# Attention and a two-layer MLP on one core: the sign of float64 weights through a Prelu, and two head pairs moved from TensorE

## The chip, the core and the metric

The kernel runs on one core of a Trainium2 chip. A core has TensorE (matrix products), VectorE, ScalarE and GpSimd (elementwise work and reductions), SyncE (it issues transfers) and 16 DMA engines. The time is device microseconds for one execution, as the median of several runs.

## What is computed

Attention with a causal mask over 4 batches, 12 heads, 448 tokens and 64 features per head, and then a two-layer MLP over the 1792 tokens. The weights `w_in` and `w_out` arrive as float64, because a float32 array was multiplied by a float64 scalar; q, k and v are float32.

```python
scores = scale * np.matmul(q, k.transpose(0, 1, 3, 2))
scores = np.where(np.triu(ones, k=1), -1e9, scores)
attn = np.exp(scores - np.max(scores, axis=-1, keepdims=True))
attn = attn / (np.sum(attn, axis=-1, keepdims=True) + 1e-09)
x = np.matmul(attn, v)                    # then (1792, 768)
h = x @ w_in                              # (1792, 2048)
out = np.maximum(0.01 * h, h) @ w_out     # (1792, 768)
```

## The kernel before

**Attention** goes by pairs of heads, 24 of them, numbered u = 0 to 23, six to a batch. For a pair, `features` brings k and q with features on partitions into a tile kq. Pairs below `TURNED` load whole rows, TensorE transposes them (line 402) and ScalarE copies the result out of PSUM (line 405). Later pairs load 32-column runs, four loads per tensor, and VectorE transposes blocks (line 394). `scores` multiplies on TensorE (lines 433 and 447, the second adds the mask). `softmax` takes the largest score of each query, which lies along partitions: ScalarE copies chunk 0 into M (line 468), VectorE takes maxima with the other three chunks (line 474, told by its helper as 251), GpSimd reduces over partitions into MR (line 476), VectorE subtracts (line 482), ScalarE takes Exp (line 489). `products` multiplies by v (line 500) and ScalarE copies the result to xu (line 506).

`finish(u)`, for every odd u, handles pairs u-1 and u. It sums the exponentials: below `ADDS` on TensorE against ones (line 520), from `ADDS` on by three adds per pair on VectorE (line 529) and a reduction per head on GpSimd (line 535). The sums go through small transfers on ScalarE's queue: to sc, to the reciprocal on VectorE (lines 546 and 547), to DRAM (scr), and back as broadcasts to rb. VectorE divides, rb = xu * rb (line 561), ScalarE takes the high part of the result (line 562) and VectorE the low part (line 563). Both parts of a batch's six pairs form the tile xt.

**Layer 1** takes three products per block, high x high, low x high, high x low, 18 per output block f and 288 per batch (line 585). ScalarE applies the leaky maximum with Prelu (line 591), and SyncE stores to DRAM as gd. **Layer 2** (line 772) reads gd back, 1176 products of 384 columns, with combined weights W and combined activations r (`combine`, lines 635 to 638).

**Weights.** `unpack` turns a float64, read as two 32-bit words, into a float32. ScalarE scales the high word, read as a float32, by 2^-112, which moves its exponent to where a shift by three bits keeps it. VectorE takes the sign from the high word (line 333), joins the top three bits of the low word to it (line 335), and shifts the scaled value left by three and joins that (line 337). It is called 16 times for `w_in`, beside attention, and 16 times for `w_out`, behind it. Each call covers 768 results per partition. A w_in value is then split into a high part wh (ScalarE, line 353) and a low part wl (VectorE, line 356).

**The order.** `Plan.emit` sets the order of all engines. It is a list scheduler with written-out durations that gives each operation a priority: the pair's number plus a number of its kind from the table `LATER`, and for the weights a line `PIECE`. Layer 1 has lower priority and fills TensorE between attention's operations; where nothing is ready TensorE gets small products on zeros (`warm`, line 321). Each engine then runs its own list strictly in order.

Of the kernel before, what the change touches and what calls it, by code (L numbers as in the profile page):

```python
# [8 lines left out]
F32 = mybir.dt.float32  # L9
# [8 lines left out]


LATER = {  # L20
    "add": 30.41, "load": 20.48, "v": 44.64, "transpose": 285.25, "features": 38.43, "scores": 30.1,
    "chunk 0": 20.56, "max": -46.8, "all max": -64.55, "subtract": 56.57, "exp": -39.38, "products": 1.84,
    "take products": 35.34, "sum all": 56.98, "sums": 1.62, "take sums": -46.21, "spread": 73.7, "invert": 43.51,
    "store": -0.31, "broadcast": 43.97, "divide": 93.42, "x hi": 58.73, "x lo": -27.08,
}

EARLY = 8

TURNED = 12

PORT = (0.78, 2.05)

PIECE = (168.2, -16.48)


SAME = -29.41


class Plan:
# [123 lines left out]
def attention_moe_kernel(  # L163
# [15 lines left out]
    nc = tc.nc  # L179
# [67 lines left out]
    def copy(out_, in_, n, r=(), w=(), prio=0.0, **kw):  # L247
        return act(n + 55, lambda: nc.scalar.activation(out=out_(), in_=in_(), func=kw.pop("func", ACTF.Copy), **kw), r, w, prio)
# [75 lines left out]
    def unpack(out_, in_, words, sign, val, R, G, V, prio, first, base, after=()):  # L324

        word = lambda j: words().bitcast(I32).rearrange("p (n t) -> p n t", t=2)[..., j]
        g = lambda: sign().bitcast(I32)
        v = lambda: val().bitcast(I32)  # L330
        dma(950, out_, in_, (base,), (R,), first, after=after)
        copy(val, lambda: word(1).bitcast(F32), DM, (R, base), (V,), prio, scale=2.0 ** -112)
        dve(DM, lambda: nc.vector.tensor_scalar(out=g(), in0=word(1), scalar1=-0x80000000, scalar2=None, op0=ALU.bitwise_and),
            (R, base), (G,), prio, 0.5, port=-1)
        dve(DM, lambda: nc.vector.scalar_tensor_tensor(
            out=g(), in0=word(0), scalar=29, in1=g(), op0=ALU.logical_shift_right, op1=ALU.bitwise_or), (R, base), (G,), prio, chain=0.03, port=-1)
        return dve(DM, lambda: nc.vector.scalar_tensor_tensor(
            out=v(), in0=v(), scalar=3, in1=g(), op0=ALU.logical_shift_left, op1=ALU.bitwise_or), (G, base), (V,), prio, chain=0.03, port=-1)

# [69 lines left out]

    order = sorted(segs)  # L410
    NTB, NM = 3, 2
    ADDS = 11
    MERGE = [lambda u: u >= 0, lambda u: u >= 99, lambda u: u >= 99]
    for tag, n, width_ in (("M", NM, S), ("MR", 1, S), ("t", NTB, 1024)):
        for i in range(n):
# [440 lines left out]
```

## Time and profile before

| | |
|---|---|
| median of 3 runs | 593.76 us (592.93 to 595.21) |
| the profiled execution | 595.98 us, of which 594.2 us are its span |
| mean granted TensorE clock | 0.996 |
| attention's last product ends | about 271.6 us into the span |
| layer 1's last product ends | about 385 us |

Layer 1's first products stand at 67.7 us, so from there to 271.6 us attention and layer 1 share TensorE. A row of a timeline gives the start, the duration of the merged instructions, the engine, the line and, in brackets, how long the engine had been idle and what released it. A row of a group gives busy time in total and the mean of one instruction.

### The profile page before, as it was taken

How to read it: one execution, taken by the hardware profiler on the slowest of the kernel's cores; microseconds unless marked ns; L12 is line 12 of the kernel's file. 1: busy time of each engine (PE TensorE's matmuls, PEld its weight loads, DVE VectorE, ACT ScalarE, POOL GpSimd, SP SyncE). 2: the span in 40 equal slices, each digit the busy share in tenths (PEclk: the TensorE clock that was granted, in tenths of full speed). 3: DMA queues.
4: the chain of work that ended last, by engine and by line, in shares of the span. 5: the costliest groups of instructions: out<-in, count | busy, mean ns of one | idle time of the engine just before them, and what ended most of it. 6: DMA issues, size and time to landing. Idle time of an engine off the chain costs nothing.

```text
span 594.2 us, 10308 instructions
## 1 busy us (share of the span) xinstructions
PE 578.8 (97%) x3747; PEld 508.5 (86%) x3747; DVE 462.7 (78%) x929; ACT 276.7 (47%) x447; POOL 162.2 (27%) x82
## 2 busy tenths in 40 slices
PE   8989899999999999999999999999999999999997
PEld 7655667878777787788999999989999999999997
DVE  4899889999999887784167899999767666666664
ACT  3778566555543543434233546654423242424331
POOL 1544234353669887897000000000000000000000
PEclk9999899999999999999999999999999999999999
DMA  8976876688556664312388766105533333232201
GB/s 168 239 182 124 175 160 189 212 190 245 141 112 125 151 131 97 94 49 94 109 312 295 258 221 201 63 17 147 154 98 99 97 99 105 90 119 77 88 14 40
DMA packets 153486, 82.90 MB, mean 140 GB/s; under 512 B 95580, under 2 KB 151388, under 8 KB 153436
## 3 DMA queue, kind: packets, MB, share of 16 engines
q1 hardware_dynamic: 146304, 76.57, 46.6%
q10 hardware_dynamic: 7132, 5.68, 3.7%
q8 instruction: 29, 0.48, 0.3%
q14 instruction: 21, 0.17, 0.1%
HBM read 61.87 MB, written 20.27 MB: 138 GB/s over the span
## 4 chain that ended last, share of the span: by engine, by line
PE 69%; DVE 15%; issue 4%; ACT 3%; DMA 3%; POOL 3%; ACTq 1%; SPq 1%; DVEq 0%; POOLq 0%
PE h L772 32%; PE h L585 27%; PE big L500 4%; PE S L433 4%; DVE M L251 3%; DVE t L482 3%; POOL MR L476 2%; DVE W L638 2%; DVE v L635 2%; DVE t L251 2%; DMA qraw<-in_q_dram 1%; DMA rb<-scr 1%; ACTq L245 1%; SPq L245 1%; DVE r L638 1%
## 5 line engine op out<-in xcount | busy, mean ns | idle before, releaser
L585 PE MATMUL h<-xt,wh 128*128 128x448 f32 x768 | 221.9, 370 | 0.5 <-DVE xt L251 0.5
L772 PE MATMUL h<-W,r 128*128 128x384 f32 x882 | 164.1, 334 | 0.1
L772 PEld LDWEIGHTS h<-W,r 128*128 128x128 f32 x882 | 153.8, 188 | 0.6 <-DVE r L638 0.4
L585 PEld LDWEIGHTS h<-xt,wh 128*128 128x128 f32 x768 | 142.5, 189 | 13.0 <-DVE xt L251 0.8
L585 PE MATMUL h<-xt,wl 128*128 128x448 f32 x384 | 140.5, 366 | 0.0
L476 POOL PARTITION_ALL_REDUCE MR<-M x48 | 80.0, 1714 | 98.7 <-DVE M L251 75.2
L535 POOL PARTITION_ALL_REDUCE t<-t x28 | 81.7, 2964 | 18.3 <-DVE t L251 14.4
L585 PEld LDWEIGHTS h<-xt,wl 128*128 128x128 f32 x384 | 72.3, 188 | 5.8
L637 ACT ACTIVATE r<-v 128x512 fp32r<-128x512 f32 x70 | 41.9, 598 | 74.3 <-DVE v L635 74.1
L482 DVE TENSOR_TENSOR t<-S,MR 128x64 f32<-128x64 f32 x192 | 67.6, 410 | 2.2 <-POOL MR L476 2.2
L638 DVE TENSOR_TENSOR r<-v,r 128x512 fp32r<-128x512 f32 x70 | 47.2, 690 | 27.4 <-ACT r L637 25.7
L489 ACT ACTIVATE t<-t 128x1024 f32<-128x1024 f32 x48 | 50.6, 1056 | 33.3 <-DVE t L482 31.5
L251 DVE TENSOR_TENSOR M<-S,M 128x320 f32<-128x320 f32 x144 | 49.0, 354 | 20.2 <-ACT M L468 10.5
L772 PE MATMUL h<-xw,r 128*128 128x384 f32 x294 | 62.5, 335 | 0.6 <-DVE r L638 0.3
L591 ACT ACTIVATE h<-h 128x448 f32<-128x448 f32 x64 | 34.3, 538 | 55.0 <-PE h L585 33.7
L433 PE MATMUL S<-kq 64*128 64x192 f32 (+3 forms) x384 | 53.1, 404 | 4.3 <-DVE t L482 4.1
L772 PEld LDWEIGHTS h<-xw,r 128*128 128x128 f32 x294 | 51.9, 188 | 1.5 <-DVE r L638 1.0
L433 PEld LDWEIGHTS S<-kq 64*128 64x128 f32 x384 | 32.9, 186 | 23.0 <-issue 11.9
L500 PE MATMUL big<-t,v 128*64 128x192 f32 (+3 forms) x384 | 47.8, 386 | 0.8 <-ACT kq L405 0.8
L635 DVE TENSOR_TENSOR v<-A 128x512 f32<-128x512 f32 x71 | 47.7, 689 | 0.0
L500 PEld LDWEIGHTS big<-t,v 128*64 128x64 f32 x384 | 26.3, 136 | 22.0 <-issue 11.7
L637 ACT ACTIVATE r<-A 128x512 fp32r<-128x512 f32 x28 | 17.7, 632 | 30.3 <-PE h L772 30.3
(87 smaller groups left out, 520.0 us busy)
## 6 DMA issues: line engine op xcount, KB each, us to landing
gd<-h SPq DMA_DIRECT2D x64, 224.0 KB
A<-gd SPq DMA_DIRECT2D x28, 512.0 KB
stage<-in_moe_w_in_dram SPq DMA_DIRECT2D x16, 768.0 KB
A<-in_moe_w_out_dram SPq DMA_DIRECT2D x16, 768.0 KB
rb<-scr ACTq DMA_DIRECT2D x48, 112.0 KB
v<-in_v_dram SPq DMA_DIRECT2D x48, 96.0 KB
kraw<-in_k_dram SPq DMA_DIRECT2D x12, 224.0 KB
qraw<-in_q_dram SPq DMA_DIRECT2D x12, 224.0 KB
```

The costliest lines, as they stand in the source:

```text
L251: return dve(n, lambda: nc.vector.tensor_tensor(out=out_(), in0=a(), in1=b(), op=op), r, w, prio, **kw)
L433: nc.tensor.matmul(out=T["S", u, bank, e][:, col:col + n], lhsT=T[kq][rows, 128 * c:128 * c + 128], rhs=T[kq][rows, S + qs:2 * S], start=c ...
L476: P.op("Pool", 1.52, lambda e=e: nc.gpsimd.partition_all_reduce(T[mr][:, e], T[m][:, e], 128, ReduceOp.max), [(*m, e)], [(*mr, e)], turn(" ...
L482: i = dve(len(es) * n, lambda c=c, qs=qs, n=n, es=es: nc.vector.tensor_tensor(out=T[t][:, cut(es), at(c):at(c) + n], in0=s(c, es), in1=T[m ...
L489: act(1024 + 55, lambda e=e: nc.scalar.activation(out=T[t][:, e], in_=T[t][:, e], func=ACTF.Exp, scale=scale), (), [(*t, e)], turn("exp", u))
L500: nc.tensor.matmul(out=bigs(key[1])[64 * e:64 * e + 64, qs:S], lhsT=T[vv][:, c, e, :], rhs=T["t", u % NTB][:, e, 512 * bank + col:512 * ba ...
L535: P.op("Pool", 2.87, lambda t=t, e=e: nc.gpsimd.partition_all_reduce(T[t][:, e, 512:512 + S], T[t][:, e, 512 - S:512], 128, ReduceOp.add), ...
L585: nc.tensor.matmul(out=T[key][:, :S], lhsT=T[w, f, 1][:, 128 * c:128 * c + 128], rhs=T["xt", b][:, x, :], start=(c == 0 and j == 0), stop= ...
L635: nc.vector.tensor_tensor(out=x(), in0=get(terms[0]), in1=get(terms[1]), op=ALU.add if terms[2] > 0 else ALU.subtract)
L637: act(n, lambda: nc.scalar.activation(out=hi(), in_=x(), func=ACTF.Copy), [*rd, *hold], [(out_cell, "h")], prio)
L638: return dve(n, lambda: nc.vector.tensor_tensor(out=lo(), in0=x(), in1=hi().bitcast(F32), op=ALU.subtract), [*rd, (out_cell, "h")], [out_c ...
L772: nc.tensor.matmul(out=T[key][:, :HO], lhsT=g()[:, jj * 128:jj * 128 + 128], rhs=W[:, w * HO:(w + 1) * HO], start=(e == 0 and jj == 0 and ...
```

## The change

`unpack` loses one VectorE operation. ScalarE's function changes from Copy to Prelu with a slope of 2^32 for negative values. A positive high word still comes out times 2^-112, a negative one times 2^-112 x 2^32 = 2^-80, so that the exponent carries one bit more. Shifted left by three, this bit lands in the sign's place, and the old sign bit drops out. VectorE then only shifts the low word right by 29 and joins. `TURNED` goes from 12 to 10, so pairs 10 and 11 are transposed by VectorE; `ADDS` goes from 11 to 9, so the sums of pairs 8 and 9 are taken by VectorE and GpSimd. All numbers of `LATER`, `PIECE` and `SAME` are others, so the whole order is made anew.

```diff
 LATER = {
-    "add": 30.41, "load": 20.48, "v": 44.64, "transpose": 285.25, "features": 38.43, "scores": 30.1,
+    "add": 150.59, "load": -94.56, "v": -49.5, "transpose": 203.33, "features": -41.49, "scores": 29.31,
...
-TURNED = 12
+TURNED = 10
...
-PIECE = (168.2, -16.48)
-SAME = -29.41
+PIECE = (324.72, -32.1)
+SAME = 30.46
...
-        copy(val, lambda: word(1).bitcast(F32), DM, (R, base), (V,), prio, scale=2.0 ** -112)
-        dve(DM, lambda: nc.vector.tensor_scalar(out=g(), in0=word(1), scalar1=-0x80000000, scalar2=None, op0=ALU.bitwise_and),
+        copy(val, lambda: word(1).bitcast(F32), DM, (R, base), (V,), prio, scale=2.0 ** -112, func=ACTF.Prelu, alpha=2.0 ** 32)
+        dve(DM, lambda: nc.vector.tensor_scalar(out=g(), in0=word(0), scalar1=29, scalar2=None, op0=ALU.logical_shift_right),
             (R, base), (G,), prio, 0.5, port=-1)
-        dve(DM, lambda: nc.vector.scalar_tensor_tensor(
-            out=g(), in0=word(0), scalar=29, in1=g(), op0=ALU.logical_shift_right, op1=ALU.bitwise_or), (R, base), (G,), prio, chain=0.03, port=-1)
         return dve(DM, lambda: nc.vector.scalar_tensor_tensor(
             out=v(), in0=v(), scalar=3, in1=g(), op0=ALU.logical_shift_left, op1=ALU.bitwise_or), (G, base), (V,), prio, chain=0.03, port=-1)
...
-    ADDS = 11
+    ADDS = 9
```

The first place is VectorE around the maxima of pair 7 (M_99; t_101 is pair 6's tile in the subtractions, rb a divide, sc and rc the sums and their inverse). Before:

```order
L482 TENSOR_TENSOR t_101<-S,MR_100 128x448
L482 TENSOR_TENSOR t_101<-S,MR_100 128x192
L482 TENSOR_TENSOR t_101<-S,MR_100 128x320
L337 SCALAR_TENSOR_TENSOR stage<-stage 128x768
L251 TENSOR_TENSOR M_99<-S,M_99 128x320
L251 TENSOR_TENSOR M_99<-S,M_99 128x192
L251 TENSOR_TENSOR M_99<-S,M_99 128x64
L251 TENSOR_TENSOR M_99<-S,M_99 128x320
L251 TENSOR_TENSOR M_99<-S,M_99 128x192
L251 TENSOR_TENSOR M_99<-S,M_99 128x64
L546 TENSOR_SCALAR sc_122<-sc_122 112x16
L547 RECIPROCAL rc_947<-sc_122 112x16
```

And in the changed kernel, whose lines from 335 on are lower by two:

```order
L480 TENSOR_TENSOR t_101<-S,MR_100 128x448
L251 TENSOR_TENSOR rb_215<-xu_639,rb_215 128x448
L480 TENSOR_TENSOR t_101<-S,MR_100 128x192
L480 TENSOR_TENSOR t_101<-S,MR_100 128x320
L251 TENSOR_TENSOR rb_123<-xu_773,rb_123 128x448
L544 TENSOR_SCALAR sc_122<-sc_122 112x16
L545 RECIPROCAL rc_930<-sc_122 112x16
L251 TENSOR_TENSOR M_99<-S,M_99 128x320
L251 TENSOR_TENSOR M_99<-S,M_99 128x192
L251 TENSOR_TENSOR M_99<-S,M_99 128x64
```

The divides of pairs 2 and 3 and the inverse now stand ahead of the maxima; before, the inverse and the divide of pair 3 came behind them.

The second place is TensorE where layer 1 begins (kraw_95 and qraw_96 are pair 9, kraw_92 and qraw_93 pair 10). Before:

```order
L402 MATMUL big<-ident,kraw_95 128x112 x4
L402 MATMUL big<-ident,qraw_96 128x112 x4
L585 MATMUL h<-xt_124,wh_1_554 128x448 x2
L585 MATMUL h<-xt_124,wl_1_829 128x448
L402 MATMUL big<-ident,kraw_92 128x112 x4
L402 MATMUL big<-ident,qraw_93 128x112 x4
L585 MATMUL h<-xt_124,wh_1_554 128x448 x2
L585 MATMUL h<-xt_124,wl_1_829 128x448
```

And in the changed kernel:

```order
L400 MATMUL big<-ident,kraw_95 128x112 x4
L400 MATMUL big<-ident,qraw_96 128x112 x4
L583 MATMUL h<-xt_125,wh_1_521 128x448 x2
L583 MATMUL h<-xt_125,wl_1_666 128x448
L583 MATMUL h<-xt_125,wh_1_521 128x448 x2
L583 MATMUL h<-xt_125,wl_1_666 128x448
```

Pair 10's transpositions are gone, and four groups of three layer-1 products follow each other.

The third place is VectorE at pair 18 (M_98 its maxima, t_101 its subtractions, rb the divides of pairs 14 and 15, xt their low parts). Before, behind the maxima and the first subtractions:

```order
L482 TENSOR_TENSOR t_101<-S,MR_100 128x64
L482 TENSOR_TENSOR t_101<-S,MR_100 128x448
L482 TENSOR_TENSOR t_101<-S,MR_100 128x192
L482 TENSOR_TENSOR t_101<-S,MR_100 128x320
L251 TENSOR_TENSOR rb_215<-xu_2061,rb_215 128x448
L251 TENSOR_TENSOR rb_123<-xu_2255,rb_123 128x448
L251 TENSOR_TENSOR xt_1968<-rb_215,xt_1968 128x448
L251 TENSOR_TENSOR xt_1968<-rb_123,xt_1968 128x448
```

And in the changed kernel:

```order
L392 STREAM_TRANSPOSE kq_2393<-qraw_93 128x448
L251 TENSOR_TENSOR M_98<-S,M_98 128x320
L251 TENSOR_TENSOR M_98<-S,M_98 128x192
L251 TENSOR_TENSOR rb_215<-xu_2062,rb_215 128x448
L251 TENSOR_TENSOR M_98<-S,M_98 128x64
L251 TENSOR_TENSOR M_98<-S,M_98 128x320
L251 TENSOR_TENSOR M_98<-S,M_98 128x192
L251 TENSOR_TENSOR rb_123<-xu_2182,rb_123 128x448
L251 TENSOR_TENSOR M_98<-S,M_98 128x64
L251 TENSOR_TENSOR xt_1879<-rb_215,xt_1879 128x448
L480 TENSOR_TENSOR t_101<-S,MR_100 128x64
```

The two divides and a low part moved from behind the subtractions to between the maxima and ahead of the subtractions.

## Rows read from the trace of the kernel before

**Rows 1.** The page's first part: busy time, share, instructions of each engine

```profile
PE 578.8 (97%) x3747; PEld 508.5 (86%) x3747; DVE 462.7 (78%) x929; ACT 276.7 (47%) x447; POOL 162.2 (27%) x82
```

**Rows 2.** The chain that ended last, in order: start, duration, engine, tile, line

```profile
271.58 91.21 PE h L585 x449
...
401.46 189.22 PE h L772 x1090
```

**Rows 3.** Windows: length, busy time of each engine, TensorE's clock, DMA share, GB/s

```profile
50.00:100.00 50.00, 45.06 (x390) 31.16 (x387) 44.63 (x103) 32.42 (x49) 16.72 (x10) 0.97 0.77 175
100.00:150.00 50.00, 50.00 (x297) 40.79 (x299) 48.75 (x87) 29.74 (x39) 21.93 (x10) 1.00 0.75 203
150.00:200.00 50.00, 48.84 (x324) 39.08 (x321) 46.29 (x107) 24.19 (x36) 37.87 (x18) 1.00 0.59 132
200.00:250.00 50.00, 49.10 (x334) 38.63 (x334) 40.57 (x100) 21.42 (x30) 41.35 (x19) 1.00 0.49 110
...
350.00:400.00 50.00, 49.45 (x254) 45.94 (x253) 48.20 (x94) 29.64 (x62) 0.00 (x0) 1.00 0.32 106
```

**Rows 4.** TensorE's timeline, transpositions of pairs 9 to 11 and one sum

```profile
66.97 1.01 PE L402 MATMUL big<-ident,qraw 112*128 112x112 f32 x4 [2.12 <-ACT xu L506]
...
68.92 0.95 PE L402 MATMUL big<-ident,kraw 112*128 112x112 f32 x4
...
70.30 0.71 PE L585 MATMUL h<-xt,wh 128*128 128x448 f32 x2
...
78.81 0.58 PE L402 MATMUL big<-ident,kraw 112*128 112x112 f32 x4
79.16 0.65 PE L585 MATMUL h<-xt,wh 128*128 128x448 f32 x2
...
96.08 1.93 PE L520 MATMUL big<-t,ones 128*32 128x448 f32 x32
97.94 1.95 PE L500 MATMUL big<-t,v 128*64 128x448 f32 x16
```

**Rows 5.** Groups: operation, shapes, count, busy us, mean ns, idle before

```profile
L535 POOL PARTITION_ALL_REDUCE t<-t x28 | 81.7, 2964 | 18.3 <-DVE t L251 14.4 <-issue 2.3 <-DVE sc L546 1.1
...
L482 DVE TENSOR_TENSOR t<-S,MR 128x64 f32<-128x64 f32 x192 | 67.6, 410 | 2.2 <-POOL MR L476 2.2
...
L251 DVE TENSOR_TENSOR M<-S,M 128x320 f32<-128x320 f32 x144 | 49.0, 354 | 20.2 <-ACT M L468 10.5 <-PE S L447 6.4
...
L591 ACT ACTIVATE h<-h 128x448 f32<-128x448 f32 x64 | 34.3, 538 | 55.0 <-PE h L585 33.7 <-DMA rb<-scr 4.8 <-issue 4.7
...
L251 DVE TENSOR_TENSOR t<-t 128x128 f32<-128x128 f32 (+2 forms) x42 | 24.2, 576 | 0.6
...
L335 DVE SCALAR_TENSOR_TENSOR stage<-stage 128x768 int32<-128x768 int32 x16 | 15.5, 969 | 0.4
...
L506 ACT ACTIVATE xu<-big 128x448 f32<-128x448 f32 x24 | 12.9, 537 | 14.5 <-PE big L500 5.3 <-DVE rb L251 4.9 <-DVE M L251 2.9
...
L394 DVE STREAM_TRANSPOSE kq<-kraw 128x448 f32<-128x448 f32 x12 | 7.6, 630 | 3.4 <-PE S L433 3.4
```

**Rows 6.** GpSimd's timeline, two pairs of sum reductions

```profile
157.70 5.73 POOL L535 PARTITION_ALL_REDUCE t<-t  x2 [1.10 <-DVE sc L546]
...
169.24 5.73 POOL L535 PARTITION_ALL_REDUCE t<-t  x2 [0.75 <-issue]
```

**Rows 7.** VectorE's timeline: divides beside reductions; the last inverse and its divides

```profile
159.75 0.61 DVE L251 TENSOR_TENSOR rb<-xu,rb 128x448 f32<-128x448 f32 x1
...
172.08 2.45 DVE L251 TENSOR_TENSOR rb<-xu,rb 128x448 f32<-128x448 f32 x1 [0.40 <-DMA rb<-scr]
...
282.01 0.25 DVE L547 RECIPROCAL rc<-sc 112x16 f32<-112x16 f32 x1
289.83 0.62 DVE L251 TENSOR_TENSOR rb<-xu,rb 128x448 f32<-128x448 f32 x1 [7.57 <-DMA rb<-scr]
292.33 0.62 DVE L251 TENSOR_TENSOR rb<-xu,rb 128x448 f32<-128x448 f32 x1 [1.88 <-DMA rb<-scr]
```

More of the change, by code (lines that the diff above doesn't have):

```diff
@@ L20 @@
 LATER = {
-    "add": 30.41, "load": 20.48, "v": 44.64, "transpose": 285.25, "features": 38.43, "scores": 30.1,
-    "chunk 0": 20.56, "max": -46.8, "all max": -64.55, "subtract": 56.57, "exp": -39.38, "products": 1.84,
-    "take products": 35.34, "sum all": 56.98, "sums": 1.62, "take sums": -46.21, "spread": 73.7, "invert": 43.51,
-    "store": -0.31, "broadcast": 43.97, "divide": 93.42, "x hi": 58.73, "x lo": -27.08,
+    "add": 150.59, "load": -94.56, "v": -49.5, "transpose": 203.33, "features": -41.49, "scores": 29.31,
+    "chunk 0": -49.05, "max": 10.85, "all max": -27.67, "subtract": 187.66, "exp": -3.99, "products": -27.02,
+    "take products": 60.68, "sum all": -67.17, "sums": -45.77, "take sums": -38.45, "spread": 91.11, "invert": 12.05,
+    "store": 14.06, "broadcast": 71.49, "divide": -54.78, "x hi": -3.74, "x lo": 57.3,
 }
 EARLY = 8
-TURNED = 12
+TURNED = 10
 PORT = (0.78, 2.05)
-PIECE = (168.2, -16.48)
-SAME = -29.41
+PIECE = (324.72, -32.1)
+SAME = 30.46
 class Plan:
```

## The prediction

> **What bounds the kernel now.** I read the busy times first: TensorE is busy for 97% of the span, VectorE for 78%, ScalarE for 47%, GpSimd for 27% [rows 1]. A mean hides stages, so the chain of waits comes next: its last pieces are layer-1 products in one run of 91.21 us and layer-2 products in one of 189.22 us [rows 2]. In these two stages only TensorE counts, and the change takes no product from either. The run of 449 also gives a unit: 91.21 / 449 = 0.203 us for a layer-1 product.
>
> Then the windows of 50 us [rows 3]. From 50 to 100 us TensorE has 4.94 us without a product, and its granted clock is 0.97, which is (1 - 0.97) x 50 = 1.5 us more lost at the lower level of 1.2 GHz. From 100 to 150 it is full, and VectorE too (48.75 of 50). From 150 to 250 TensorE misses 1.16 + 0.90 us, from 350 to 400 0.55 us. So behind 50 us there are about 9.1 us that less waiting could give, 6.4 of them between 50 and 100 us. VectorE is the engine that attention waits for there: 44.63 us of 50, with GpSimd at 16.72 and ScalarE at 32.42 [rows 3]. The largest single gap is the 2.12 us ahead of pair 9's transposition of q; TensorE waits for ScalarE's copy xu to free a bank, and the rows behind it run at the lower clock [rows 4].
>
> **The change part by part.**
>
> *The sign through Prelu.* Each of the 32 unpackings loses one scalar_tensor_tensor of 969 ns; the tensor_scalar that stays keeps its shape and only reads the other word [rows 5]. For w_in that is 16 x 0.969 = 15.5 us of VectorE, for w_out as much again. On ScalarE a Copy becomes a Prelu. The trace has both on 448 columns out of PSUM, 538 ns against 537 [rows 5], so the price is nothing within 0.1 us. The order of the changed program has one table load, as before, so no reload stands between Prelu and Exp.
>
> *Two pairs turned by VectorE.* Pairs 10 and 11 lose their four transpositions on TensorE. Pair 10's two took from 68.92 to 70.30, 1.38 us at the low clock; one of pair 11's took from 78.81 to 79.16, 0.35 us, with its loads hidden under neighbouring products [rows 4]. Together 1.38 + 2 x 0.35 = 2.1 us of TensorE. VectorE gets 4 x 0.630 = 2.5 us [rows 5]. ScalarE loses four copies, which nobody waits for once the bank is not needed. SyncE issues four loads of 32-column runs for each of these tensors instead of one; every such load of the trace had landed before VectorE wanted it, since the engine's waits ahead of line 394 are for score products alone, so I take nothing, and in the worst case a late load is part of the upper bound.
>
> *Two pairs summed by GpSimd.* The sums for pairs 8 and 9 leave TensorE: 97.94 - 96.08 = 1.86 us [rows 4]. VectorE gets six adds of 576 ns, 3.5 us, and GpSimd four reductions of 2964 ns, 11.9 us [rows 5], in a stretch where it is busy for 21.93 of 50 us [rows 3], so they find room.
>
> Sum on TensorE: 2.1 + 1.86 = 3.9 us less work, in stretches where it is full or is the engine that is waited for. Sum on VectorE during attention: 15.5 - 2.5 - 3.5 = 9.5 us less, and VectorE paces the stretch up to 150 us. So waits can close there, by no less than nothing and by no more than the 6.4 us they are.
>
> *Which waits close.* Up to pair 6 TensorE's order is nearly that of before, and what VectorE saves on the joins is spent at once on low parts and transpositions moved up, so I count nothing for the opening. At pair 7 there is a visible gain: divides 2 and 3 and the inverse now stand ahead of the six maxima, as the order shows, where divide 3 stood behind them. The copy of xu, queued on ScalarE behind the high part that needs this divide, comes sooner; the 2.12 us gap goes, and with it the low clock that follows it, 1.5 us [rows 3, 4]. From the first layer-1 product on, weights are ready earlier: the order has 216 products ahead of the scores of pair 12, where before there were 144. I count 2.1 + 1.5 = 3.6 us, between the ends 0 and 6.4.
>
> *The later pairs.* In the order of the changed program layer-1 products stand in blocks of 30 and 42 between pairs (30 before), 657 before the last product of attention, not 594. Two pairs together then have 72 x 0.203 = 14.6 us of layer 1 beside their own products, against 60 x 0.203 = 12.2 us, so TensorE leaves VectorE 1.2 us more for a pair whose VectorE work hardly changes. The 2.1 us missed from 150 to 250 could shrink; but the divides have moved between the maxima (third place of the order), where they can wait. I take the two as cancelling.
>
> *Layer 2's weights.* With 63 products fewer behind attention there are 12.8 us less to hide the unpacking of w_out under, and the unpacking is 15.5 us shorter. VectorE is busy for 48.20 of 50 us there [rows 3], so without the saving the 12.8 us would be paid nearly in full. I take nothing, from -0.5 (the 0.55 us gap goes) to +2.
>
> The sum: 594.2 - 3.9 - 3.6 = 586.7 us of span. The profiled execution took 595.98 us, 1.8 more than its span and 2.2 more than the median 593.76 of the runs; I take the difference of 7.5 us from the median: **586.3 us**.
>
> **Rivals.**
>
> *Only TensorE's own work goes.* Some other wait takes the place of the 2.12 us: the inverse now waits ahead of the maxima for the sums' transfer, or low parts arrive late. For it speaks that VectorE and TensorE stay equally dense from 100 to 150 us [rows 3]. Time: 593.8 - 3.9 = 589.9.
>
> *VectorE was the whole cause.* All 6.4 us of the early stretch and the 2.1 us behind it close: 593.8 - 3.9 - 8.5 = 581.4. Against it: the same gaps follow each pair's chain through ScalarE and GpSimd, which does not get shorter.
>
> *The sums on GpSimd hold VectorE up.* One divide took 2.45 us; it began at 172.08 while two reductions ran from 169.24 on. Another, begun at 159.75 within the reductions that started at 157.70, took 0.61 us [rows 6, 7]. So a reduction can cost VectorE 2.45 - 0.61 = 1.84 us but mostly costs nothing. Four more, in a place with many two-input operations, cost 0 to 7.4 us; at 7.4 VectorE keeps 2.1 of its 9.5 us, and the time is 593.8 - 2.1 = 591.7. The quick divide beside a running reduction is why it gets a small chance.
> The Trainium skill (SBUF — State Buffer, "Who interferes with whom") says that a VectorE instruction with two SBUF inputs contends with a GpSimd instruction that reads SBUF, and that the loser fully blocks for the whole instruction. By that rule alone the four reductions could hold VectorE for 4 x 2.96 = 11.9 us, more than the change saves it, and the time would stay near that of before. The divide of 172.08 agrees with it, the one of 159.75 does not.
>
> *Slower: the moved divides wait for their broadcast.* In the trace the first divide of a late batch ran 289.83 - 282.01 = 7.8 us behind the start of its reciprocal, the second 10.3 us [rows 7]. In the changed order one add, six subtractions, two transpositions and two maxima stand between, 0.58 + 6 x 0.41 + 2 x 0.63 + 2 x 0.354 = 5.0 us of VectorE work [rows 5], and up to the second divide a divide and three maxima more, 6.7 us. If score products and copies fill no time, each of the five places (pairs 14, 16, 18, 20, 22) waits for 3.6 us, with the maxima, the reduction and the next scores behind it: 18 us, less some 0.5 us of slack a place, 15.5; the time is 586.3 + 15.5 = 601.8. It decides for slower from (7.5 + 2.5) / 5 = 2 us a place on. Against it: a scores product and a copy also lie between, and the divides of the trace stand at another place, where broadcasts had no hurry.
>
> *Prelu is dearer than Copy.* It would have to be so from SBUF alone. ScalarE is idle for half of the span [rows 1], and 0.1 us on 32 operations hides; no case of its own.
>
> **How the numbers follow.** The forecast of 586.3 (584 to 589) gets 0.55; only TensorE's work 0.18; all waits closed 0.10; GpSimd in VectorE's way 0.10; moved divides 0.07. The range reaches to half of each neighbour: 581 to 592. 0.5% of 593.76 is 3.0 us, about what a measurement of this kernel can tell from no change. Faster by more than that means below 590.8: the forecast, all waits closed, and two thirds of the 589.9 case, 0.77. Within: the rest of that case and the GpSimd case, 0.16. Slower: 0.07.
>
> **What would show it.** In the profile of the changed kernel each weight matrix should have 16 scalar_tensor_tensor operations instead of 32, and VectorE some 25 us less busy time; the Prelu of 768 columns should last as long as the Copy did. TensorE should show no gap over 1 us ahead of pair 9's q, and a clock near 1.00 from 50 to 100 us. The 100 to 250 us windows should stay above 49 of 50. Wrong would be: waits of the divides for rb between maxima of a microsecond or more each (the slower case), subtractions or low parts of 2 us beside reductions (GpSimd), or a layer-2 start that waits for line 638.

## The result, and the profile after

The changed kernel took 598.55 us (median of 18 runs, 594.16 to 603.50) and the kernel before, run beside it, 594.17 us (18 runs). The ratio is 1.0055, with a 95% interval of 1.0031 to 1.0079. Once more on another chip it was 599.23 against 594.21 us, ratio 1.0087 (1.0058 to 1.0116). The ratios here and below leave out runs that fell in a slower state, such as the one of 603.50 us, and are not the quotients of the medians. By the medians the change costs 4.4 and 5.0 us, by the ratios 3.3 and 5.2. The forecast of 586.3 us, and its whole range, were on the other side. The profiled execution took 600.16 us with a span of 598.3 us.

The first part of its page (busy time, share, instructions) answers to [rows 1]:

```profile
PE 577.2 (96%) x3690; PEld 507.2 (85%) x3690; DVE 436.5 (73%) x907; ACT 274.6 (46%) x442; POOL 174.5 (29%) x86
```

VectorE is 26.2 us less busy, as the prediction had it, and TensorE 1.6 us, and yet the span grew. Two groups of its page (count, busy us and mean ns, idle before) show the new unpacking, the Prelu on ScalarE and the one join left on VectorE:

```profile
L335 DVE SCALAR_TENSOR_TENSOR stage<-stage 128x768 int32<-128x768 int32 x16 | 15.4, 965 | 3.2 <-ACT stage L248 2.5
...
L248 ACT ACTIVATE stage<-stage 128x768 f32<-128x768 f32 x16 | 14.5, 912 | 15.0 <-DVE wl L354 8.5 <-DMA stage<-in_moe_w_in_dram 4.4 <-DMA qraw<-in_q_dram 2.0
```

The operations cost what was forecast: 965 ns for the join (969 before), 912 for the Prelu (919 for the Copy before). The windows of 50 us (length, busy time of PE, PEld, DVE, ACT, POOL, then TensorE's clock as a share of full speed, DMA share and GB/s) answer to [rows 3]:

```profile
0.00:50.00 50.00, 43.16 (x503) 31.99 (x505) 33.65 (x103) 28.95 (x42) 17.40 (x16) 0.93 0.75 175
50.00:100.00 50.00, 44.15 (x353) 31.79 (x347) 40.22 (x100) 29.09 (x45) 17.39 (x10) 0.97 0.76 175
100.00:150.00 50.00, 47.63 (x283) 38.84 (x284) 44.22 (x85) 30.46 (x40) 26.53 (x11) 1.00 0.81 211
150.00:200.00 50.00, 47.50 (x312) 37.41 (x311) 41.66 (x98) 22.79 (x34) 37.91 (x18) 1.00 0.55 125
200.00:250.00 50.00, 50.00 (x326) 40.57 (x325) 37.40 (x96) 20.29 (x30) 37.44 (x18) 1.00 0.46 112
```

From 200 us on TensorE is full. Before that it is idle for 6.84 + 5.85 + 2.37 + 2.50 = 17.6 us, and its clock is 0.93 and 0.97 in the first two windows, which loses some (0.07 + 0.03) x 50 = 5 us. In the kernel before, the window from 100 to 150 us was full and the one behind it missed 1.16 us [rows 3]; its first window was

```profile
0.00:50.00 50.00, 45.75 (x542) 33.04 (x542) 38.34 (x115) 31.93 (x46) 18.87 (x18) 1.00 0.80 184
```

The changed kernel's longest gaps on TensorE, from its timeline (start, duration, operation, idle time before and who ended it):

```profile
39.23 1.01 PE L400 MATMUL big<-ident,qraw 112*128 112x112 f32 x4 [3.63 <-ACT kq L403]
...
70.46 0.60 PE L400 MATMUL big<-ident,qraw 112*128 112x112 f32 x4 [0.49 <-ACT xu L504]
72.25 0.65 PE L583 MATMUL h<-xt,wh 128*128 128x448 f32 x2 [1.19 <-DVE t L480]
...
101.71 0.47 PE L583 MATMUL h<-xt,wl 128*128 128x448 f32 x1 [3.05 <-DVE wl L354]
```

VectorE's timeline beside them, the inverse of the sums (line 544), the maxima (M, line 251) and a divide (rb):

```profile
29.89 1.42 DVE L480 TENSOR_TENSOR t<-S,MR 128x64 f32<-128x64 f32 x4 [0.17 <-POOL MR L474]
33.96 0.17 DVE L544 TENSOR_SCALAR sc<-sc 112x16 f32<-112x16 f32 x1 [2.65 <-DMA sc<-sr]
...
34.75 2.18 DVE L251 TENSOR_TENSOR M<-S,M 128x320 f32<-128x320 f32 x6
36.84 0.97 DVE L354 TENSOR_TENSOR wl<-stage,wh 128x768 fp32r<-128x768 f32 x1
...
67.85 0.17 DVE L544 TENSOR_SCALAR sc<-sc 112x16 f32<-112x16 f32 x1 [1.80 <-DMA sc<-sr]
...
68.22 2.13 DVE L251 TENSOR_TENSOR M<-S,M 128x320 f32<-128x320 f32 x6
...
93.84 1.00 DVE L251 TENSOR_TENSOR M<-S,M 128x64 f32<-128x64 f32 x3
97.17 0.63 DVE L251 TENSOR_TENSOR rb<-xu,rb 128x448 f32<-128x448 f32 x1 [2.33 <-DMA rb<-scr]
...
100.70 0.95 DVE L354 TENSOR_TENSOR wl<-stage,wh 128x768 fp32r<-128x768 f32 x1
```

At 31.3 us VectorE is done with pair 2's subtractions. TensorE is making the scores of pair 3, and in the kernel before their maxima stood ahead of the inverse. Now the inverse of finish(1) stands ahead of them and waits 2.65 us for the transfer of the sums. The rows of ScalarE show how that reaches TensorE:

```profile
28.25 1.18 ACTq L245 DMA_DIRECT2D sc<-sr  x1
...
37.84 0.90 ACT L248 ACTIVATE stage<-stage 128x768 f32<-128x768 f32 x1 [1.95 <-DVE wl L354]
38.65 0.53 ACT L403 ACTIVATE kq<-big 128x448 f32<-128x448 f32 x1
```

The maxima end at 36.9, a low part wl follows to 37.8, ScalarE's unpacking copy has waited for that one (it overwrites what wl reads), the copy kq is queued behind it, and TensorE needs the bank that kq empties: 3.63 us of gap at 39.23, with a clock of 0.73 from 40 to 50 us. The same at 67.85 (1.80 us), and at 97.17 a divide waits 2.33 us for its broadcast between pair 9's maxima, and TensorE 3.05 us for the low part wl behind it. The chain that ended last names the three transfers, where that of the kernel before names no transfer of sums or of broadcasts ahead of 167.91 us:

```profile
28.25 5.68 DMA sc<-sr
...
63.16 4.66 DMA sc<-sr
...
91.01 6.07 DMA rb<-scr
```

### The profile page after: what moved, and what is told of

Read it like the earlier page. It is cut to its first block, busy times and chain, and to the rows that moved or that the text cites. A ratio compares the mean times of both kernels' runs of the same rounds, so it can differ in the third digit from the quotient of the medians.

```text
span 598.3 us, 10194 instructions
## 1 busy us (share of the span) xinstructions
PE 577.2 (96%) x3690; PEld 507.2 (85%) x3690; DVE 436.5 (73%) x907; ACT 274.6 (46%) x442; POOL 174.5 (29%) x86
## 4 chain that ended last, share of the span: by engine, by line
PE 74%; DVE 10%; DMA 9%; issue 2%; POOL 2%; ACT 2%; ACTq 1%; SPq 0%; DVEq 0%; POOLq 0%
PE h L770 33%; PE h L583 30%; PE S L431 5%; PE big L498 3%; DMA rb<-scr 3%; DVE M L251 2%; DMA stage<-in_moe_w_in_dram 2%; DMA sc<-sr 2%; POOL t L533 2%; DMA qraw<-in_q_dram 1%; DVE t L480 1%; DVE wl L354 1%; DMA gd<-h 1%; PE big L400 1%; DVE stage L335 1%
## 5 line engine op out<-in xcount | busy, mean ns | idle before, releaser
L533 POOL PARTITION_ALL_REDUCE t<-t x32 | 93.1, 2957 | 23.4 <-issue 11.5
L431 PE MATMUL S<-kq 64*128 64x448 f32 (+3 forms) x384 | 54.2, 416 | 4.8 <-DVE t L480 4.2
L466 ACT ACTIVATE M<-S 128x896 f32<-128x896 f32 (+1 forms) x27 | 22.2, 834 | 28.4 <-PE S L445 19.0
```

The costliest lines, as they stand in the source:

```text
L431: nc.tensor.matmul(out=T["S", u, bank, e][:, col:col + n], lhsT=T[kq][rows, 128 * c:128 * c + 128], rhs=T[kq][rows, S + qs:2 * S], start=c ...
L533: P.op("Pool", 2.87, lambda t=t, e=e: nc.gpsimd.partition_all_reduce(T[t][:, e, 512:512 + S], T[t][:, e, 512 - S:512], 128, ReduceOp.add), ...
```

## Theory and rivals

**Theory.** The new order puts VectorE instructions that wait for small transfers ahead of work that TensorE needs; each engine runs its list strictly in order, so the wait is paid by TensorE, and behind the gap the clock is lower. The unpacking itself is a gain. **Rivals.** The unpacking is the loss, since it starts weight loads sooner and these hold the small transfers up. Or: moving waits only moves the gaps. Or: the two pairs cost more on VectorE than they save on TensorE.

In some kernels a few lines were added to `Plan.emit` that take named instructions out of the finished list and put them at another place; the rest of the order stays word for word. The reciprocal and the store behind an inverse move with it, and since the list is one for all engines, the store moves on ScalarE's queue as well. The cuts below show the moves alone, without these lines.

## Experiments on the order

**The inverses put back behind the maxima**, the changed kernel with

```diff
+    P.moves = [([("inverse", 1)], "behind", ("maxima", 3)), ([("inverse", 5)], "behind", ("maxima", 7))]
```

> The changed kernel with two instructions put back: the inverse of finish(1), with its store, stands behind the maxima of pair 3 on VectorE, and that of finish(5) behind the maxima of pair 7, as before the change; all else is unchanged. Theory (VectorE, which takes its instructions in order, now stands still for the sums' transfer ahead of maxima that TensorE needs): the waits of 2.65 us at 33.96 and 1.80 us at 67.85 in the changed kernel's trace go, the first layer-1 product starts 3 to 4.5 us sooner than at 72.25, TensorE's clock between 40 and 50 us (0.73) comes near 1, and the time is 593 to 595 us against 598.5 of the changed kernel. Rival (the loss is in the faster unpacking, that pulls the stage loads ahead, or elsewhere than in this order): the first maxima start sooner but wait for something else, and the time stays within 1.5 us of 598.5.

595.95 us, ratio 1.0041 (1.0020 to 1.0062), between the two times expected. Beside the changed kernel on one chip:

> The changed kernel itself, as the yardstick for the run beside it: 597 to 600 us.

> The changed kernel with the inverses of finish(1) and finish(5) behind the maxima of pairs 3 and 7. If the inverses carry a good part of the loss: 2 to 4 us below the yardstick. If the waits only change places (TensorE's gap at 39.23 shrinks from 3.63 to 1.36 us, but the gap of 2 us ahead of pair 9's q is back) and the divides carry it: within 1 us of the yardstick.

599.23 us and 595.88 us: the two inverses cost 3.4 us, and the intervals of the two ratios, 1.0058 to 1.0116 and 0.9999 to 1.0053, do not overlap. VectorE and TensorE in the trace of the first run with the inverses moved:

```profile
32.39 2.18 DVE L261 TENSOR_TENSOR M<-S,M 128x320 f32<-128x320 f32 x6
34.49 0.18 DVE L559 TENSOR_SCALAR sc<-sc 112x16 f32<-112x16 f32 x1
...
64.83 0.19 DVE L559 TENSOR_SCALAR sc<-sc 112x16 f32<-112x16 f32 x1
```

```profile
37.19 0.60 PE L410 MATMUL big<-ident,qraw 112*128 112x112 f32 x4 [1.36 <-ACT kq L413]
...
67.04 0.60 PE L410 MATMUL big<-ident,qraw 112*128 112x112 f32 x4 [1.99 <-ACT xu L518]
```

Behind the maxima no inverse waits. TensorE's first gap falls from 3.63 to 1.36 us, and the second place loses its wait but gets back the gap ahead of pair 9's q that the kernel before had [rows 4], 1.99 us here.

**Two divides as well**, those of pairs 6 and 7, behind pair 9's last subtraction:

```diff
+    P.moves += [([("divide", 6), ("divide", 7)], "behind", ("subtract", 9))]
```

> The first run's kernel, and besides the divides of pairs 6 and 7 moved behind pair 9's last subtraction on VectorE, so that the wait of 2.33 us at 97.17 for the broadcast doesn't stand ahead of the subtractions and of the unpacked weights that TensorE's first project product waits for (gap of TensorE at 101.71, waiting 3.05 us). Theory (waits in order on VectorE): 2 to 3 us less than the first run's kernel, 590 to 593 us. Rival (the weights are late for another reason, the sum of late divides then holds the layer's end): within 1 us of the first run's kernel or above it.

593.03 us against 595.95 on the same chip, 2.9 us less. TensorE's gap ahead of the layer-1 product, 3.05 us in the changed kernel, was 2.00 us with the inverses moved,

```profile
96.06 0.47 PE L601 MATMUL h<-xt,wl 128*128 128x448 f32 x1 [2.00 <-DVE wl L364]
```

and with the divides moved too it is

```profile
94.21 0.48 PE L601 MATMUL h<-xt,wl 128*128 128x448 f32 x1 [0.41 <-DVE wl L364]
```

So two inverses and two divides at other places take some 6 us from the changed kernel by these runs. Run once more on another chip (below, 594.34 us), the same kernel had a ratio of 1.0002 where it has 0.9966 here, so that by the ratios it is 3 to 7 us.

The clock's part shows in all executions and not only in the profiled ones. The mean granted clock was 0.9934 and 0.9943 over the two groups of runs of the changed kernel, 0.9955 and 0.9966 with the inverses moved, 0.9983 and 0.9974 with the divides moved too, and 0.9986 over the 137 runs of the kernel before that stood beside the experiments. From the changed kernel to the one before that is (0.9986 - 0.9934) x 598 = 3.1 us at most, an estimate: much of the loss may reach the time as lost clock.

**The opposite: the kernel before with the inverses ahead of the maxima.**

```diff
+    P.moves = [([("inverse", 1)], "ahead", ("maxima", 3)), ([("inverse", 5)], "ahead", ("maxima", 7))]
```

> The kernel before with nothing changed but the place of two instructions: the inverses of finish(1) and finish(5), with their stores, stand ahead of the maxima of pairs 3 and 7 on VectorE, as the changed kernel has them. Theory (the place of the inverse is what costs): VectorE waits at both, 2 us or more together, TensorE's clock falls after the gap, and the time rises by 3 to 5 us, to 597 to 599 us against 594.2. Rival (the transfer is late only in the changed kernel, because its faster unpacking has asked for two stage loads ahead of it): the inverse finds its sums there, waits under 0.7 us at each place, and the time stays within 1 us of 594.2.

597.43 us against 594.11, ratio 1.0049 (1.0026 to 1.0072). VectorE and TensorE:

```profile
31.66 0.96 DVE L345 SCALAR_TENSOR_TENSOR stage<-stage 128x768 int32<-128x768 int32 x1
32.54 0.17 DVE L561 TENSOR_SCALAR sc<-sc 112x16 f32<-112x16 f32 x1
...
63.67 0.17 DVE L561 TENSOR_SCALAR sc<-sc 112x16 f32<-112x16 f32 x1 [2.12 <-DMA sc<-sr]
```

```profile
67.83 1.01 PE L412 MATMUL big<-ident,qraw 112*128 112x112 f32 x4 [3.06 <-ACT xu L520]
```

The place alone costs 3.3 us, and the trace puts it at finish(5): there the inverse waits 2.12 us, the gap that was 2.12 us [rows 4] is 3.06, and the clock from 70 to 80 us is 0.81 where it was 0.98. At finish(1) the inverse does not wait at all. Theory and rival were each right at one place. In the old order two unpacking operations (1.5 us) lie ahead of that inverse, and the transfer, issued from 29.59 on, was there by 32.54; in the changed kernel, issued from 28.25 on, it was not there before 33.96.

**A weight load behind the inverse.** SyncE's rows show what differs. In the changed kernel two loads of 768 KB leave together (the second ends its issue at 27.80, just ahead of the sums). It is the order that brings them together: with the old unpacking put back into it (below) they still leave as a pair from 24.37 us on, and with the new unpacking in the old order they leave at 24.37 and 33.23. One is moved:

```diff
+    P.moves = [([("stage", 3)], "behind", ("inverse", 1))]
```

> The changed kernel with one DMA issue moved: the load of the fourth weight block (768 KB), that SyncE issues at about 27 us just ahead of the first sums' transfer of 7 KB (issued at 28.25), is issued behind the loads of v and of the queries that follow, at 31 us or later. If that load holds the small transfer up: the sums are there by 32.5 us instead of 33.96, the first inverse waits under 1.5 us instead of 2.65, and the time falls by 1 to 2 us, to 596.5 to 597.5. If the place of the inverse alone counts: the wait stays at 2.3 us or more and the time within 0.7 us of 598.5.

SyncE's issues in the changed kernel:

```profile
24.96 2.84 SPq L245 DMA_DIRECT2D stage<-in_moe_w_in_dram  x2
```

and with the one load moved, then VectorE's inverse and ScalarE's queue in that kernel:

```profile
25.09 0.68 SPq L255 DMA_DIRECT2D stage<-in_moe_w_in_dram  x1
...
32.03 0.44 SPq L255 DMA_DIRECT2D stage<-in_moe_w_in_dram  x1
```

```profile
31.80 0.16 DVE L565 TENSOR_SCALAR sc<-sc 112x16 f32<-112x16 f32 x1
```

```profile
28.83 1.18 ACTq L255 DMA_DIRECT2D sc<-sr  x1
...
37.32 0.90 ACT L258 ACTIVATE stage<-stage 128x768 f32<-128x768 f32 x1 [2.60 <-DMA stage<-in_moe_w_in_dram]
38.12 0.52 ACT L416 ACTIVATE kq<-big 128x448 f32<-128x448 f32 x1
```

The load did hold the small transfer up. Without it the inverse starts at most 31.80 - 28.83 = 3.0 us after the issue began, without waiting, instead of 33.96 - 28.25 = 5.7 us. But the time is 600.87 us, not less. Now ScalarE's copy of that weight block waits 2.60 us for the later load, and kq behind it: TensorE's gap is still 2.52 us, and the weights that are late at 97.85 to 101.71 in the changed kernel are later still (a gap of 4.94 us). One wait was taken away and another stood ready behind it.

**ScalarE's queue too**: the four moves, and besides the store of finish(5)'s inverses behind the next xu, and one unpacking copy behind another xu.

```diff
+    P.moves += [([("store", 5)], "behind", ("take products", 6)),
+                ([("unpack copy", 3)], "behind", ("take products", 2))]
```

> The kernel with inverses and divides put behind (593.0 us), and two instructions more on ScalarE's queue: the store of the fifth pair's inverses behind the copy of the next pair's products out of PSUM, and the unpacking copy of the fourth block behind the third pair's copy of products. In that kernel's trace ScalarE stands still for 1.84 us at 65.4 behind the store, which waits for VectorE's reciprocal, and TensorE's gap of 2.06 us at 66.69 waits for the copy queued behind it; likewise the gap of 1.31 us at 36.95. Theory (any in-order queue on which a wait for the sums stands ahead of the next pair's work costs what it waits): 2 to 3.5 us less, 589.5 to 591 us, faster than both kernels. Rival (the gaps only move to the next instruction): within 1 us of 593.0.

593.02 us, ratio 0.9970. Without these two moves the ratio was 0.9966 on one chip and 1.0002 on another, so no gain can be told. The gap of 2.06 us ahead of pair 9's q is gone, and

```profile
67.42 0.65 PE L611 MATMUL h<-xt,wh 128*128 128x448 f32 x2 [2.06 <-DVE t L500]
```

is the same 2.06 us one instruction later, now ended by VectorE's subtractions. At this place the rival holds: ScalarE's wait lay beside VectorE's own work of the same length.

## Experiments on the parts

**The unpacking alone, in the old order.** Every instruction keeps its place; the dropped join leaves a hole:

```diff
-        copy(..., scale=2.0 ** -112)
+        copy(..., scale=2.0 ** -112, func=ACTF.Prelu, alpha=2.0 ** 32)
-        tensor_scalar(... word(1), -0x80000000, bitwise_and)
+        tensor_scalar(... word(0), 29, logical_shift_right)
-        scalar_tensor_tensor(... word(0), 29, g, logical_shift_right, bitwise_or)
```

> The kernel before with the new unpacking and nothing else: every instruction stands where it stood, ScalarE's Copy becomes the Prelu, and the dropped VectorE join leaves its place empty. Theory (the new unpacking is a gain and the new order is the loss): VectorE is about 25 us less busy, the maxima and subtractions of the opening start sooner, and the time is 588 to 592 us against 594.2. Rival (the unpacking is no gain: it starts the stage loads sooner, and these hold the small transfers up): 593 to 598 us, with VectorE or ScalarE waiting longer for sums and broadcasts than before.

590.85 us against 594.91, ratio 0.9934 (0.9912 to 0.9957). On another chip, with three more kernels beside it:

> The old order with the new unpacking, once more, on one chip with the three that follow, as their common yardstick: 590 to 592 us.

592.50 against 594.37, ratio 0.9954 (0.9933 to 0.9976). The unpacking is a gain of 2 to 4 us, so it isn't the loss. It did not close the gap that the prediction wanted closed, as TensorE's timeline and the windows of the first of these runs show:

```profile
66.85 0.60 PE L401 MATMUL big<-ident,qraw 112*128 112x112 f32 x4 [2.12 <-ACT xu L505]
```

```profile
50.00:100.00 50.00, 44.66 (x393) 30.83 (x392) 42.76 (x102) 33.63 (x51) 16.33 (x11) 1.00 0.78 177
...
150.00:200.00 50.00, 50.00 (x325) 39.99 (x326) 45.36 (x110) 23.16 (x34) 40.77 (x19) 1.00 0.57 131
```

The gap is 2.12 us as before. In this pair of traces the difference lies in the clock behind it (0.97 before, 1.00 here), but not in the runs: the 25 runs of the kernel before beside it have a mean clock of 0.998, these 12 have 0.999, and among the runs at 0.999 or more the medians are still 594.1 and 591.0 us. From 150 to 200 us the 1.16 us are no longer missing [rows 3], but from 200 to 250 us 1.20 us are, where it was 0.90. So the gain is measured, and where it comes from is not shown.

**The old unpacking in the new order**, the join put back behind the sign instruction, nothing else:

> The changed kernel's order, pairs and tables, every instruction in its place, but the old unpacking: ScalarE copies, and VectorE makes the join that the change dropped, right behind the sign instruction. Theory (the unpacking itself is a gain): VectorE is about 26 us busier, half or less of it in the opening where TensorE waits for VectorE, and the time is 601 to 605 us against 598.5. Rival (VectorE waits for transfers anyway, so that its work there is hidden): within 1.5 us of 598.5.

614.59 us, ratio 1.0323 (1.0292 to 1.0354), some 10 us above the range expected. Together with the run above this is a square: old order 594.9 and 590.9 us (old and new unpacking), new order 614.6 and 598.6, the last one from another chip. The new order, with the turned pairs and the sums on GpSimd that belong to it, costs 20 us with the old unpacking and 7 to 8 us with the new one. It leans on VectorE being light: with the joins back, TensorE waits for the subtractions of two pairs,

```profile
122.19 3.34 PE L433 MATMUL S<-kq 64*128 64x448 f32 x16 [2.09 <-DVE t L482]
...
147.92 4.01 PE L433 MATMUL S<-kq 64*128 64x448 f32 x16 [5.74 <-DVE t L482]
```

**The order planned anew.** Two kernels let the planner run again with one thing changed: the kernel before with the new unpacking, and the changed kernel with the sums' transfer planned 2.3 us longer.

> The kernel before with the new unpacking alone (Prelu, one VectorE join less); the numbers that the order is planned from, the turned pairs and the pairs that GpSimd sums are those of before, and the order is planned anew with them. Theory (the unpacking itself is a gain of about 26 us of VectorE's time, and only the order drawn with it costs): the same or faster than before, 588 to 594 us, unless the newly planned order puts an inverse or a divide ahead of maxima too, which the trace will show. Rival (the unpacking is itself the loss, by ScalarE or by what it starts sooner): 597 to 600 us, with no VectorE wait for the sums ahead of maxima.

> The changed kernel with one number of its plan changed and the order planned anew: the transfer of the sums is planned as 2.3 us longer (about 4.5 us, as the changed kernel's trace shows it behind a weight load, instead of 2.3). If a wrong duration in the plan is what puts the inverses ahead of the maxima, and the rest of the order stays as good: 593 to 596 us, with no wait over 0.7 us of an inverse ahead of maxima. Rival (the tables of priorities fit one order only, and any order planned anew with them is worse): 600 us or more, like the kernel of before planned anew with the new unpacking (603.9).

603.88 us and 602.44 us (1.0158 and 1.0119). In the first three inverses wait for their sums, 1.10 us at 32.52, 1.11 at 63.72 and 0.96 at 85.87, the first of them ahead of maxima, so this plan has the same fault. In the second the first inverses no longer wait, but divides now wait 2.02 and 3.24 us for broadcasts at 51.18 and 83.02. The rival holds: the tables fit one plan, and a single better number in it was no gain by itself. That the unpacking is worth -2 to -4 us in a fixed order and +9.8 us planned anew says how much of any such comparison is the order.

**Pairs 10 and 11 turned by VectorE in the old order.**

> The kernel with the new unpacking in the old order (590.85 us), and pairs 10 and 11 turned by VectorE in that same order: TensorE's four transpositions are gone, VectorE's block transpositions stand where the four copies out of PSUM stood on ScalarE, and SyncE issues four loads of 32-column runs where one stood. The term of the prediction for this part was 2.1 us of TensorE's work. If it comes out where TensorE is full: 588.3 to 589.3 us. Rival (the transpositions lay beside waits, or the four more VectorE operations stand ahead of maxima and cost there what TensorE saves): 590.3 to 592 us.

596.90 us, which says nothing on the part: in that order the loads of pairs 12 and 13 stood ahead of the transpositions, so that these turned other data and waited for later loads (6.08 us at 74.24). With the transpositions and those loads behind the subtractions of pairs 8 and 9, and then with the inverse of finish(7) behind these as well:

> Pairs 10 and 11 turned by VectorE in the old order with the new unpacking, as in the run before, but VectorE's block transpositions stand behind the subtractions of pairs 8 and 9, where the column-run loads (which VectorE waited 6.08 us for at 74.24 in that run) have had time to land, and the loads of pairs 12 and 13 stand behind them. Theory (the part is worth TensorE's 2.1 us where no instruction waits ahead of other work): no wait of VectorE over 1 us at the transpositions and 588.3 to 590 us against 590.85 with the new unpacking alone. Rival (TensorE's transpositions lay in time that TensorE spends waiting for the pair's chain anyway, so that taking them away only lengthens the waits): 590.3 to 592 us.

> The kernel of the run beside it, and the inverse of finish(7), that waits 2.18 us at 80.5 among the subtractions of pair 8 in the trace of the new unpacking in the old order, with its store moved behind these subtractions and the transpositions of pair 10. Theory (a wait on VectorE ahead of subtractions costs what it waits as far as TensorE waits for these): TensorE's gaps of 0.35 and 0.46 us at 81.4 and 84.2 close, 0.5 to 1 us less than the run beside it. Rival (layer-1 products fill TensorE there, so that nothing is gained): within 0.5 us of it.

592.87 us (0.9973) and 591.90 us (0.9944). These ran on another chip than the unpacking alone, and the difference is within the intervals, so all were run once more side by side:

> The same with pairs 10 and 11 turned by VectorE, behind the subtractions of pairs 8 and 9. If TensorE's 2.1 us of transpositions come out: 1.5 to 2.5 us below the yardstick. If the pair's chain sets the pace there: within 1 us of it or above.

> The same with the inverse of finish(7) behind the subtractions of pair 8 as well. If a wait ahead of subtractions costs here: 0.5 to 1.5 us below the kernel with the turned pairs alone, and with them 2 to 3.5 us below the yardstick. Rival: level with it.

> The changed kernel with the inverses of finish(1) and finish(5) and the divides of pairs 6 and 7 put behind. Since its trace still has TensorE idle for 3.0 us between 100 and 200 us, where the old order with the new unpacking has none, and its TensorE has less to do by the two pairs: 1 to 3 us above the yardstick. Rival (the four moves undo the whole loss, and the two pairs then show as a gain): 2 to 4 us below the yardstick.

Beside 592.50 us for the unpacking alone: 592.31 with the turned pairs, 590.34 with the inverse moved too, 594.34 for the changed kernel with its four moves. By themselves the turned pairs brought nothing that can be told from zero: the ratio is 0.9954 without them and 0.9962 with them. Page and TensorE's timeline of the first kernel with them:

```profile
PE 574.2 (98%) x3731; PEld 504.1 (86%) x3731; DVE 437.1 (74%) x901; ACT 274.6 (47%) x443; POOL 160.8 (27%) x82
```

```profile
101.02 2.11 PE L451 MATMUL S<-kq 64*128 64x448 f32 x16 [1.86 <-DVE t L501]
```

TensorE is busy for 576.1 - 574.2 = 1.9 us less than with the unpacking alone, at mean clocks of 1.000 and 0.999. But the scores of pair 11 now wait 1.86 us for subtractions, a gap that the unpacking alone did not have. VectorE's rows show what most of it is. The inverse of finish(9) stands between these subtractions; with the turned pairs and without them it runs as

```profile
99.80 0.17 DVE L566 TENSOR_SCALAR sc<-sc 112x16 f32<-112x16 f32 x1 [1.22 <-DMA sc<-sr]
```

```profile
100.46 0.24 DVE L545 TENSOR_SCALAR sc<-sc 112x16 f32<-112x16 f32 x1
```

VectorE reaches the subtractions 2.0 us sooner with the turned pairs (97.17 against 99.13 us), the transfer of the sums is issued only 0.4 us sooner (97.4 against 97.8), and so the inverse waits for 1.22 of the 1.86 us (0.60 of 1.24 us in a second trace of this kernel). It is the fault of the changed kernel again, at another place. Whether the turned pairs are a gain with this inverse moved was not tried.

With the inverse of finish(7) moved as well the kernel took 2.0 us less here and 1.0 us less on the chip before. The trace that called for this move had that inverse waiting 2.18 us, at 80.50, but without the turned pairs; with them it finds its sums there in both traces (76.46 and 78.47 us). So what the move takes away is not shown. This kernel is the fastest of all, ratio 0.9919 (0.9896 to 0.9942) on one chip and 0.9944 (0.9920 to 0.9969) on the other: 3 to 5 us below the kernel before by the ratios, and 7 to 10 us below the changed one.

The mended kernel, as the changed one with its four moves is called from here, stays 1.8 us above the unpacking alone. Its first trace (span 590.1 us) has TensorE idle for

```profile
100.00:150.00 50.00, 48.87 (x286) 40.40 (x284) 46.83 (x91) 30.45 (x42) 25.58 (x12) 1.00 0.83 216
150.00:200.00 50.00, 48.10 (x325) 37.77 (x321) 39.24 (x94) 21.70 (x32) 38.50 (x17) 1.00 0.54 119
```

1.13 + 1.90 = 3.0 us where the old order with the new unpacking has none; that one misses 1.20 us from 200 to 250 us, where the mended kernel is full. In the stretch from 100 to 200 us a divide runs 2.41 us beside a sum reduction on GpSimd and pair 13's maxima come behind it; whether that is the whole of it was not tried.

## Why the prediction was wrong, step by step

**VectorE's saving** was right: 26.2 us against some 25, a Prelu no dearer than the Copy.

**TensorE's own work, -3.9 us.** The work went: from 576.1 us (old order, new unpacking) to 572.9 us busy (new order, mended), both at full clock, 3.2 us (a second trace of the old order has 575.3, so 2.4 to 3.2). The step "in stretches where it is full or is the engine that is waited for" is where the term failed. Measured alone, the turned pairs' 2.1 us of work came out as 0.2 us of time by the medians and none by the ratios: in the trace TensorE then waits 1.86 us for subtractions, 1.22 of them behind an inverse that waits for its sums.

**"I count nothing for the opening"** is the step that failed most. The order was read for what stands where, and costed by VectorE's busy time; what was not asked is when the data of a moved instruction arrive. The opening lost 2.6 us of TensorE's time (6.84 us idle against 4.25 in the old kernel's first 50 us) and 0.07 x 50 = 3.5 us of clock.

**"Which waits close", -3.6 us.** At pair 7 the prediction called it a visible gain that the inverse stands ahead of the maxima. The gap ahead of pair 9's q did go, from 2.12 [rows 4] to 0.49 us. But VectorE paid 1.80 us for it at 67.85, and the first layer-1 product starts at 72.25 instead of 67.66. In the kernel before, the same move costs 3.3 us. The sign of the step was wrong. Its 1.5 us of clock were also mis-sized, as they came from a single execution at 0.996: of the 137 runs of the kernel before, 86 had a mean clock of 0.999 or 1.000, and their mean of 0.9986 loses only 0.0014 x 594 = 0.8 us in the whole span.

**The later pairs and layer 2's weights** were taken as cancelling, and did roughly: 150 to 200 us lost 1.34 us more than before [rows 3], 200 to 250 and 350 to 400 closed 0.90 and 0.55. What the prediction did not have is the window from 100 to 150, which was full and lost 2.37 us: mostly the late low part behind pair 7's divide, at 97.17.

**The rivals.** "Only TensorE's own work goes" named the mechanism, the inverse waiting ahead of the maxima and low parts arriving late, and both came. Its price was wrong: it let the new wait do no more than take the place of the closed one, 589.9 us, with nothing on the other side. The slower rival had the right kind, divides waiting for broadcasts between maxima, but at pairs 14 to 22; there the changed kernel waits 0.15 us at 174.58 and TensorE is full from 200 us on. GpSimd in VectorE's way: one divide of 2.36 us at 157.32, as there was one of 2.45 before [rows 7].

**The sum as the runs give it**: the unpacking -2 to -4 us, the turned pairs 0, the two inverses +3.4, the two divides +2.9, and some +1.8 left in the new order, together +4 to +6; measured +4.4 and +5.0 by the medians. The mended kernel's two ratios, 0.9966 and 1.0002, are 2 us apart, so no part is known better than that. The +1.8 and the sums by GpSimd were not taken apart.

## What to carry to other kernels

When an order is made anew, look in it for each instruction that waits for a transfer and ask what stands behind it on its engine; a count of busy time says nothing of that, and two such instructions of 0.17 us cost 3.4 us here. Judge a cheaper operation in a fixed order first: the same unpacking was -2 to -4 us in place and +9.8 us with the order planned anew. Work taken from the busiest engine is no gain yet where it only brings an engine sooner to a wait for a transfer: 2 us less of it here, and 1.22 us more of waiting. And one profiled execution does not size what the clock costs; the clocks of all runs do.

## What the runs showed of the hardware that was not expected

A transfer of 7 KB on ScalarE's queue was late behind a 768 KB load on SyncE's queue: 5.7 us from its issue to the instruction that waits, against at most 3.0 us with that load issued later. The Trainium skill (DMA: Bandwidth & Descriptors, "Queues, rings and completion order") says that a DMA engine takes turns between its queues, a packet at a time. From that rule alone one would not expect a load on another queue to hold so small a transfer back for long. Here it held it for over 2 us, and no run tells whether data movement or completion took them.

The clock punishes a gap unevenly, in the same kernel too. The old order with the new unpacking and the turned pairs was profiled twice: a gap of 2.12 us ahead of 65.79 was followed by full clock (1.00 from 50 to 100 us), one of 2.13 us ahead of 66.33 by the lower level (0.97, with 0.50 from 68 to 70 us). The kernel before had its 2.12 us ahead of 66.97 and the lower level behind it (0.97) in its profiled run, though most of its runs kept a mean clock of 0.999 or more.
